# Attention followed by a mixture of experts: the attention's tiles in phases of three pairs, and GpSimd's indirect stores behind spaced operations

## The chip, the core and the metric

The kernel runs on one core of a Trainium2 chip. The core has a matrix engine (TensorE, PE in the views), VectorE (DVE), ScalarE (ACT), GpSimd (POOL), and SyncE (SP), which here issues DMAs. Each engine takes its own instructions in its own order, and the engines wait for each other by semaphores. The metric is device time in microseconds of one execution, as a median of several runs. Times inside an execution come from one profiled run and count from the start of its span.

## What is computed

Two parts follow each other. The first is a gated linear attention over 4 batches, 8 heads, 768 positions and a head size of 48. Each position has a complex gate, and a state of 48 x 48 per head is turned, damped and added to:

```python
mag = np.sqrt(a_re * a_re + a_im * a_im)
scale = np.minimum(mag, 0.999) / (mag + 1e-06)
a_re_n, a_im_n = (a_re * scale, a_im * scale)
for t in range(S):
    new_re = ar * S_re - ai * S_im
    new_im = ar * S_im + ai * S_re
    S_re, S_im = (new_re + kv, new_im)
    y[:, :, t] = np.einsum('bhd,bhde->bhe', q[:, :, t], S_re)
```

Its output, 3072 tokens of 384 numbers, is the input of the second part, a mixture of 8 experts with two layers (384 to 1024 to 384). A noisy gate picks two experts for each token:

```python
noisy_logits = logits + noise_scale * noise
top2 = np.argpartition(-noisy_logits, 2, axis=1)[:, :2]
for e in range(E):
    for k in range(2):
        mask = top2[:, k] == e
        h = np.maximum(x[mask] @ w1[e], 0.0)
        out[mask] += top2_w[mask, k, None] * (h @ w2[e])
```

## The kernel before, in words

The attention works on 24 tiles of 128 positions. Tile n belongs to batch b = n mod 4 and tile group g = n div 4, so a group has one tile of each batch and the state goes from group to group. Tiles 2m and 2m+1 make pair m, 0 to 11. The gate's magnitude and angle are handled in pairs, the rest by tile:

- load_a, load_qk, load_v (L485 to L497): DMAs on SP for a pair's gates (re, im) and a tile's q, k and v.
- p1(m) (L505): ScalarE's Ln and Exp with VectorE's products give the log of the magnitude. p2a(m) (L520) is the Arctan, p2carry(m) (L524) adds on VectorE the angle that the group before left in car, p2t(n) (L530) makes prefix sums of the angles on TensorE (cum), rounds them on ScalarE and VectorE into tf and sends tf's last row by DMA to car (L544). p2s(m) (L546) takes Abs and two Sines: tr.
- p3(n) (L557): prefix sums of the logs on TensorE, two Exps on ScalarE (ee), qk times ee on VectorE. p3q(n, i) (L571): VectorE's products qk times tr, which give qh (i = 0) and kh (i = 1).
- tr_unit(n, i) (L577): eight transposes on TensorE into ptr and ScalarE's copy of ptr to qT or kT. sc_unit (L586): scores psc on TensorE, masked by VectorE into am. st_unit, st_upd, st_scale (L598 to L626): the state, z. y_unit (L628): TensorE's pY from z and am, ScalarE's xT; for b = 0 GpSimd opens xr, a buffer of the group's rows (three of them).
- x_unit(n) (L648): transposes back, ScalarE's copy to xr.
- glog, gturn, gsel, gdis, gscat (L656 to L747) are the gates of a group of tiles: logits, a transpose, the choice of two experts (its Exp and Ln on ScalarE), the slot of each token in its expert's list (counts on TensorE, pos and at last the reduction sl at L707 on VectorE), and gscat, which writes the rows of xr by GpSimd's indirect DMA to the slots in xs, two stores for each tile (L715). gscat3_0_4 stands for group 3, tiles 0 to 4 (exclusive); its eight stores are .0 to .7. The groups 4 and 5 go in two parts, 0_3 and 3_4.

The experts' part then reads xs by expert and runs mm1 (ph, or psc where the attention's banks are used, L966), ScalarE's and VectorE's evictions to h (L968, L971), and mm2 (po, L1002). The first pieces of it are mixed into the attention's last tiles; x_T (L926 to L949) and load_w (w1h, w2h, L870) get its operands ready.

ScalarE holds one table at a time, for Exp and Ln or for Arctan and Sine. phase(i, ...) (L464) puts each activation into a numbered phase, even for Exp and Ln, odd for the other, and loads the table at the phase's first use (L467). All of ScalarE's activations of phase i stand between the loads of i and i+1. phase_of(m) gives the phase of a pair.

The order is written out by hand in three tables. EMIT is the order in which the steps are written, so the order of buffers. ORDER holds for PE, ACT, DVE and SP a list of tokens, which is that engine's own order; a token is a step with its numbers and a count of its runs of instructions on that engine, as p2s10.1. PACE (L249) adds waits: the first instruction of one token waits for the last of another. POOL has no list; its order comes out when the kernel is built, from EMIT and the waits.

Of the kernel before, what the change touches and what calls it, by code (L numbers as in the profile page):

```python
# [37 lines left out]
    load_a2 load_qk0 load_qk1 load_a3 load_qk2 p11 p12 p30 p31 load_v0 consts2 load_qk3 p2a0 p2a1 p2t0 p2a2 p2t1  # L38
    load_a4 p2t2 p2t3 p2s0 load_v1 load_qk4 p2s1 p32 load_v2 p3q0_0 load_qk5 load_qk6 tr_unit0_0 p2carry2 p3q1_1
    load_qk7 p13 load_v3 p3q0_1 p3q1_0 load_qk8 tr_unit0_1 p14 p33 load_a5 st_unit0 p2t4 st_upd0 tr_unit1_0 p2t5  # L40
    tr_unit1_1 p3q2_1 sc_unit0_0 st_unit1 p2a3 sc_unit0_1 y_unit0 p3q2_0 clear_out7 tr_unit2_0 clear_out1 p2a4
    load_qk9 p2carry3 p2t6 p2carry4 p2t7 st_upd1 p2s2 sc_unit1_0 p3q3_1 tr_unit2_1 sc_unit1_1 p3q3_0 st_unit2 load_v4
    p2s3 p34 sc_unit2_0 st_upd2 tr_unit3_0 p35 sc_unit2_1 load_a6 y_unit1 p36 tr_unit3_1 load_v5 p3q4_0 y_unit2 p15
    st_unit3 p3q5_0 p37 st_upd3 tr_unit4_0 p3q4_1 sc_unit3_0 p16 p2t8 p3q5_1 tr_unit4_1 load_v6 p2t9 load_a7 st_unit4
    load_qk10 sc_unit3_1 y_unit3 sc_unit4_0 tr_unit5_0 sc_unit4_1 tr_unit5_1 x_unit0 p2a5 glog0_0_4 clear_out9 p3q6_0
    clear_out4 load_qk11 p2carry5 x_unit1 p2s4 load_v7 p2t10 st_scale0 p2t11 st_scale3 y_unit4 st_scale2 sc_unit5_0
    st_scale1 gturn0_0_4 load_v8 tr_unit6_0 p2s5 p3q6_1 x_unit2 load_qk12 sc_unit5_1 st_upd4 y_unit5 p2a6 st_unit5
    p3q7_0 p38 gsel0_0_4 p3q7_1 tr_unit6_1 st_upd5 p39 load_a8 p2carry6 p310 load_qk13 st_unit6 p17 p3q8_0 sc_unit6_0
    p3q8_1 tr_unit7_0 sc_unit6_1 y_unit6 p18 p311 tr_unit7_1 p2t12 sc_unit7_0 st_upd6 tr_unit8_0 load_v9 p2t13 x_unit3
    load_v10 sc_unit7_1 clear_out8 st_unit7 tr_unit8_1 x_unit4 y_unit7 st_upd7 p3q9_1 sc_unit8_0 load_a9 p2a7  # L50
    sc_unit8_1 p3q9_0 load_v11 x_unit5 tr_unit9_0 p2s6 p2carry7 clear_out0 st_unit8 load_qk14 st_scale4 p2t14
    tr_unit9_1 st_scale7 p2t15 p3q10_0 glog1_0_4 clear_out10 sc_unit9_0 y_unit8 p2a8 p3q11_0 p2s7 p2carry8 gturn1_0_4
    tr_unit10_0 st_upd8 p312 p3q10_1 p2t16 sc_unit9_1 st_unit9 st_scale5 p313 load_a10 p2t17 tr_unit10_1 p314
    clear_out5 clear_out2 y_unit9 load_qk15 st_scale6 sc_unit10_0 p19 p3q11_1 load_qk16 load_qk17 x_unit6 load_v12
    tr_unit11_0 gdis0_0_4 gsel1_0_4 p110 sc_unit10_1 p3q12_0 y_unit10 x_unit7 tr_unit11_1 gscat0_0_4 p315 load_a11
    sc_unit11_0 st_upd9 tr_unit12_0 x_unit8 sc_unit11_1 clear_out6 st_unit10 y_unit11 st_upd10 load_v13 p2a9 p3q12_1
    st_unit11 p3q13_0 tr_unit12_1 st_upd11 glog2_0_4 load_qk18 p2carry9 load_qk19 load_v14 p2s8 sc_unit12_0
    tr_unit13_0 p3q13_1 gturn2_0_4 p2t18 st_scale8 p2t19 p2a10 tr_unit13_1 sc_unit12_1 st_unit12 y_unit12 p3q14_0 p2s9
# [1472 lines left out]
```

## Time and profile before

| what | us |
|---|---|
| median of three runs (683.65 to 687.44) | 686.25 |
| the profiled execution's own time | 686.77 |
| its span in the profile | 685.1 |
| TensorE busy in the span | 650.1 |
| VectorE busy | 435.1 |
| ScalarE busy | 367.9 |
| GpSimd busy | 174.9 |

The span lies within the execution's own time. Busy time leaves out waiting; a busy TensorE need not be at its peak, since matmuls are pipelined. Shares over the whole span are means over an attention part, up to about 268 us, and an experts' part, with other limits in each. The granted clock of TensorE stands in the views as a share of its higher level of 2.4 GHz: 1.00 is that, 0.50 is 1.2 GHz, and numbers between are means over a stretch. "remote" or "another core or an unknown queue" as a releaser means that the profile found no event that ended the wait; "issue" means that the engine waited for nothing that the profile shows.

### The profile page before, as it was taken

How to read it: one execution, taken by the hardware profiler on the slowest of the kernel's cores; microseconds unless marked ns; L12 is line 12 of the kernel's file. 1: busy time of each engine (PE TensorE's matmuls, PEld its weight loads, DVE VectorE, ACT ScalarE, POOL GpSimd, SP SyncE). 2: the span in 40 equal slices, each digit the busy share in tenths (PEclk: the TensorE clock that was granted, in tenths of full speed). 3: DMA queues.
4: the chain of work that ended last, by engine and by line, in shares of the span. 5: the costliest groups of instructions: out<-in, count | busy, mean ns of one | idle time of the engine just before them, and what ended most of it. 6: DMA issues, size and time to landing. Idle time of an engine off the chain costs nothing.

```text
span 685.1 us, 14285 instructions
## 1 busy us (share of the span) xinstructions
PE 650.1 (95%) x5505; PEld 573.5 (84%) x5505; DVE 435.1 (64%) x971; ACT 367.9 (54%) x610; POOL 174.9 (26%) x183
## 2 busy tenths in 40 slices
PE   8999999997989788999999999999999999999995
PEld 3468786876878577989899899899899899899895
DVE  7899999987778547546556526735735736746411
ACT  6999999987646345264423622732632732723300
POOL 3000000135230426002513302152142142163311
PEclk9999999999899889999999999999999999999998
DMA  6937766758386555278654756698598697682201
GB/s 240 295 113 205 212 158 211 199 177 258 118 249 182 184 165 171 87 252 236 173 159 118 264 143 203 198 192 223 189 166 250 193 186 228 194 219 91 83 36 35
DMA packets 120012, 124.24 MB, mean 181 GB/s; under 512 B 73610, under 2 KB 99104, under 8 KB 119936
## 3 DMA queue, kind: packets, MB, share of 16 engines
q1 hardware_dynamic: 110672, 95.76, 48.4%
q0 software_dynamic: 9264, 27.48, 13.3%
q8 instruction: 45, 0.74, 0.4%
q14 instruction: 31, 0.25, 0.1%
HBM read 70.11 MB, written 42.90 MB: 165 GB/s over the span
## 4 chain that ended last, share of the span: by engine, by line
PE 77%; DVE 11%; ACT 4%; another core or an unknown queue 2%; DMA 2%; issue 2%; SPq 1%; POOL 0%; POOLq 0%; ACTq 0%
PE ph L966 29%; PE po L1002 24%; PE po L1027 6%; PE ptr L583 3%; PE psc L593 2%; PE cum L533 2%; PE pY L642 2%; PE pY L644 1%; PE psc L966 1%; DVE qk L565 1%; DVE am L594 1%; DVE qh L573 1%; PE cum L652 1%; DVE im L528 1%
## 5 line engine op out<-in xcount | busy, mean ns | idle before, releaser
L966 PE MATMUL ph<-x,w1h 128*128 128x512 f32 (+4 forms) x720 | 184.7, 345 | 0.0
L1002 PE MATMUL po<-w2h,h 128*128 128x384 f32 x640 | 164.2, 335 | 0.0
L966 PEld LDWEIGHTS ph<-x,w1h 128*128 128x128 f32 x720 | 125.2, 188 | 14.9 <-DVE x L949 0.2
L987 POOL DMA_INDIRECT out_dram<-ao,ox x54 | 58.0, 1073 | 258.4 <-DVE ao L1015 155.4
L966 PE MATMUL ph<-x,w1l 128*128 128x512 f32 (+4 forms) x360 | 123.9, 344 | 0.0
L1002 PEld LDWEIGHTS po<-w2h,h 128*128 128x128 f32 x640 | 115.8, 188 | 0.3
L968 ACT ACTIVATE h<-ph 128x512 fp32r<-128x512 f32 (+4 forms) x120 | 60.7, 511 | 101.0 <-PE ph L966 82.2
L971 DVE SCALAR_TENSOR_TENSOR h<-ph,h 128x512 fp32r<-128x512 f32 (+5 forms) x128 | 69.3, 548 | 60.2 <-ACT h L968 55.3
L1002 PE MATMUL po<-w2l,h 128*128 128x384 f32 x320 | 107.0, 334 | 0.0
L715 POOL DMA_INDIRECT xs<-xr,sl x48 | 54.1, 1127 | 201.7 <-DVE kh L573 127.3
L1015 DVE SCALAR_TENSOR_TENSOR ao<-po,gw,ao 128x384 f32<-128x384 f32 (+1 forms) x42 | 25.7, 612 | 101.5 <-PE po L1002 101.3
L966 PEld LDWEIGHTS ph<-x,w1l 128*128 128x128 f32 x360 | 67.6, 188 | 7.6
L948 ACT CAST x<-xj 128x512 fp32r<-128x512 f32 (+4 forms) x39 | 20.7, 531 | 87.1 <-DVE xj L945 86.2
L978 POOL DMA_INDIRECT ao<-out_dram,ox x47 | 54.5, 1160 | 32.5 <-issue 28.8
L1002 PEld LDWEIGHTS po<-w2l,h 128*128 128x128 f32 x320 | 60.1, 188 | 0.2
L593 PEld LDWEIGHTS psc<-qT,kT 112*64 112x64 f32 x768 | 37.6, 143 | 5.9 <-issue 3.9
L593 PE MATMUL psc<-qT,kT 112*64 112x128 f32 (+1 forms) x768 | 41.1, 257 | 1.1 <-ACT kT L584 0.6
L644 PE MATMUL pY<-am,v 128*48 128x128 f32 x384 | 37.2, 277 | 5.0 <-issue 2.3
L594 DVE TENSOR_TENSOR am<-psc,mask 128x512 f32<-128x512 f32 x48 | 32.3, 680 | 13.6 <-PE psc L593 7.2
L1027 PE MATMUL po<-h,w2h 128*128 128x272 f32 (+2 forms) x192 | 38.7, 294 | 0.0
L949 DVE TENSOR_TENSOR x<-xj,x 128x512 fp32r<-128x512 f32 (+4 forms) x39 | 22.6, 579 | 24.1 <-ACT x L948 24.1
L584 ACT ACTIVATE kT<-ptr 112x1024 f32<-112x1024 f32 x24 | 24.8, 1032 | 22.7 <-remote 14.8
(246 smaller groups left out, 1113.4 us busy)
## 6 DMA issues: line engine op xcount, KB each, us to landing
raw<-in_moe_w_dram SPq DMA_DIRECT2D x24, 512.0 KB
raw<-in_moe_w_dram SPq DMA_DIRECT2D x32, 384.0 KB
qk<-in_qk_dram SPq DMA_DIRECT2D x24, 384.0 KB
v<-in_v_dram SPq DMA_DIRECT2D x24, 288.0 KB
xgb<-xs SPq DMA_DIRECT2D x8, 800.0 KB
xp<-xp SPq DMA_DIRECT2D x7, 768.0 KB
re<-in_a_dram SPq DMA_DIRECT2D x12, 384.0 KB
im<-in_a_dram SPq DMA_DIRECT2D x12, 384.0 KB
```

What stands on the lines that cost most here:

```text
L593: nc.tensor.matmul(p[o:o + 64, j, z:], KT[n][:, h, z:z + 64], QT[n][:, h, z:], start=True, stop=True, skip_group_check=True)
L594: nc.vector.tensor_mul(AM[n][:, 4 * half:4 * half + 4, :].rearrange("p (a r) t -> p a (r t)", r=2), p.rearrange("p (a r) t -> p a (r t)", ...
L644: nc.tensor.matmul(o, V[n][:, H + h // 2 if h % 2 else h, :], AM[n][:, h, :], start=not g, stop=True, skip_group_check=True)
L715: d = nc.gpsimd.indirect_dma_start(out=xs, out_offset=bass.IndirectOffsetOnAxis(ap=sl[:, kk, b:b + 1], axis=0), in_=XR[g][:, lo + b, :], i ...
L966: nc.tensor.matmul(p[:, :n], W1[e, kk][i][:, f * 128:(f + 1) * 128], XW[w, kk][:, j, :], start=(c == 0), stop=(c == len(ms) - 1))
L968: highs.append(nc.scalar.activation(h[:, 0:n], p[:, :n], AF.Relu))
L971: d = nc.vector.scalar_tensor_tensor(h[:, dst:dst + b - a], p[:, a:b], 0.0, h[:, a:b].bitcast(F32), op0=OP.max, op1=OP.subtract)
L978: nc.gpsimd.indirect_dma_start(out=ao[j][0:w, :], out_offset=None, in_=out, in_offset=bass.IndirectOffsetOnAxis(ap=OX[e][0:w, j:j + 1], ax ...
L987: d = nc.gpsimd.indirect_dma_start(out=out, out_offset=bass.IndirectOffsetOnAxis(ap=OX[e][0:n, j:j + 1], axis=0), in_=a, in_offset=None, b ...
L1002: nc.tensor.matmul(p[:, :DM], HT[w, f][i][:, o:o + 128], W2[f // 2][k2][:, f % 2, :], start=(m == 0), stop=(m == len(ms) - 1))
L1015: kept.append(nc.vector.scalar_tensor_tensor(a, p[0:n, :DM], g, a, op0=OP.mult, op1=OP.add))
L1027: nc.tensor.matmul(p[:, :n], W2[f // 2][k2][:, f % 2, kk * 128:(kk + 1) * 128], HT[0, f][i][:, 0:n], start=(m == 0), stop=(m == len(ms) - 1))
```

## The change

Pairs go three to a phase and not two, after a first phase of three in both; the phases of Sines, Exps of ee and gates follow:

```diff
     def load_a(m):
-        RE[m] = pf.tile([128, 2, HD], F32, name="re", bufs=4)
-        IM[m] = pf.tile([128, 2, HD], F32, name="im", bufs=4)
+        RE[m] = pf.tile([128, 2, HD], F32, name="re", bufs=5)
+        IM[m] = pf.tile([128, 2, HD], F32, name="im", bufs=5)
...
     def phase_of(m):
-        return 0 if m < NP0 else 2 * ((m - NP0 + 2) // 2)
+        return 2 * (m // 3)
+
+
+    def turn_phase(m):
+        return 1 if m < 2 else min(2 * ((m + 1) // 3) + 1, 7)
...
-        phase(2 * (2 * m // B) + 1, flat(TR[m][:, 0]), a, AF.Sin, scale=-TWO_PI, bias=b_cos)
-        phase(2 * (2 * m // B) + 1, flat(TR[m][:, 1]), f, AF.Sin, scale=-TWO_PI)
+        phase(turn_phase(m), flat(TR[m][:, 0]), a, AF.Sin, scale=-TWO_PI, bias=b_cos)
+        phase(turn_phase(m), flat(TR[m][:, 1]), f, AF.Sin, scale=-TWO_PI)
...
-        ph = 2 * g + 2 if n > 1 else 0
+        ph = 2 * ((n + 4) // 6) if n > 1 else 0
...
-                   lambda *a: phase(2 * min(g + 3, NG), *a),
+                   lambda *a: phase((4, 6, 6, 8, 8, 8)[g], *a),
```

Phases 0 to 12 become 0 to 8, so 13 table loads become 9. EMIT and ORDER are written anew up to about tile 19, to match; the experts' part keeps its order. In PACE the three waits of TensorE stay, and GpSimd's stores get other ones. Before, the stores of groups 0 to 2 stand in orders of their own (.1, .3, .6, .7 and so on for group 0), and some stores have no such wait; after, they stand as .0, .1, .2, and each later one has its own operation of ScalarE or VectorE. Only the last store of group 5's first part (gscat5_0_3.5) now stands behind those of its second part. The rows for group 3 and the first of group 4:

```diff
 PACE = {
...
-    ("POOL", "gscat2_0_4.3"): ("ACT", "y_unit17.0"), ("POOL", "gscat3_0_4.1"): ("ACT", "tr_unit19_0.0"),
-    ("POOL", "gscat3_0_4.0"): ("ACT", "load_w10.0"), ("POOL", "gscat3_0_4.5"): ("ACT", "glog4_0_3.0"),
-    ("POOL", "gscat3_0_4.3"): ("ACT", "gsel4_0_3.1"), ("POOL", "gscat3_0_4.7"): ("ACT", "x_T0_0_1.0"),
-    ("POOL", "gscat3_0_4.2"): ("ACT", "gsel4_0_3.2"), ("POOL", "gscat3_0_4.6"): ("ACT", "x_unit18.0"),
...
+    ("POOL", "gscat2_0_4.7"): ("DVE", "p3q19_1.0"), ("POOL", "gscat3_0_4.1"): ("ACT", "x_T0_0_1.0"),
+    ("POOL", "gscat3_0_4.2"): ("ACT", "x_T0_0_2.0"), ("POOL", "gscat3_0_4.3"): ("DVE", "gsel4_0_3.14"),
+    ("POOL", "gscat3_0_4.4"): ("ACT", "mm10_0_1.0"), ("POOL", "gscat3_0_4.5"): ("DVE", "st_scale17.0"),
+    ("POOL", "gscat3_0_4.6"): ("ACT", "y_unit20.0"), ("POOL", "gscat3_0_4.7"): ("ACT", "tr_unit22_1.0"),
+    ("POOL", "gscat4_0_3.0"): ("ACT", "y_unit21.0"), ("POOL", "gscat4_0_3.1"): ("DVE", "gsel4_3_4.11"),
```

Line numbers of after are two to five higher than those of before. ScalarE before, the phase of the Arctans of pairs 3 and 4, from its table load to the next. im is the angle, tr<-tf are Sines (tf, small where a bias is given):

```order
L467 ACT_TABLE_LOAD
L468 ACTIVATE im<-im 128x768
L584 ACTIVATE qT<-ptr 112x1024
L645 ACTIVATE xT<-pY 128x512
L468 ACTIVATE tr<-tf 128x768
L468 ACTIVATE im<-im 128x768
L538 ACTIVATE tf<-cum,small 128x384 x2
L468 ACTIVATE tr<-tf,small 128x768
L584 ACTIVATE kT<-ptr 112x1024
L468 ACTIVATE tr<-tf,small 128x768
L468 ACTIVATE tr<-tf 128x768
L467 ACT_TABLE_LOAD
```

ScalarE after, the phase of the Arctans of pairs 3 to 5, its first rows:

```order
L469 ACT_TABLE_LOAD
L470 ACTIVATE tr<-tf,small 128x768
L470 ACTIVATE tr<-tf 128x768
L470 ACTIVATE im<-im 128x768 x2
L650 ACTIVATE xT<-pY 128x512
L589 ACTIVATE qT<-ptr 112x1024
L543 ACTIVATE tf<-cum,small 128x384 x2
L470 ACTIVATE im<-im 128x768
L589 ACTIVATE kT<-ptr 112x1024
L470 ACTIVATE tr<-tf,small 128x768
L543 ACTIVATE tf<-cum,small 128x384 x2
L470 ACTIVATE tr<-tf 128x768
```

And on to the next load:

```order
L555 ACTIVATE tf<-tf 128x768
L650 ACTIVATE xT<-pY 128x512
L589 ACTIVATE qT<-ptr 112x1024
L543 ACTIVATE tf<-cum,small 128x384
L470 ACTIVATE tr<-tf,small 128x768
L470 ACTIVATE tr<-tf 128x768
L543 ACTIVATE tf<-cum,small 128x384
L469 ACT_TABLE_LOAD
```

Between two loads stood 11 operations with two Arctans; now 21 with three stand there, and three pairs of Sines.

GpSimd before, the stores of group 3 (sl_2899) and the first of group 4, with what each waits for by engine or DMA queue:

```order
L715 DMA xs<-xr,sl_2899 24576x400 [waits DVE_49,Activation_49,Pool_49]
L715 DMA xs<-xr,sl_2899 24576x400
L715 DMA xs<-xr,sl_2899 24576x400 [waits Activation_49]
L715 DMA xs<-xr,sl_2899 24576x400 x5
L715 DMA xs<-xr,sl_3339 24576x400 [waits DVE_49,DMASW0_49,Activation_49,Pool_49]
L715 DMA xs<-xr,sl_3339 24576x400 [waits DMASW1_49]
L715 DMA xs<-xr,sl_3339 24576x400 [waits DMASW2_49]
```

GpSimd after, the same stores (sl_2895 is group 3's, sl_3335 that of group 4):

```order
L720 DMA xs<-xr,sl_2895 24576x400 [waits DVE_49,Activation_49,Pool_49]
L720 DMA xs<-xr,sl_2895 24576x400 [waits Activation_49] x2
L720 DMA xs<-xr,sl_2895 24576x400 [waits DVE_49]
L720 DMA xs<-xr,sl_2895 24576x400 [waits Activation_49]
L720 DMA xs<-xr,sl_2895 24576x400 [waits DVE_49]
L720 DMA xs<-xr,sl_2895 24576x400 [waits Activation_49] x2
L720 DMA xs<-xr,sl_3335 24576x400 [waits DVE_49,DMASW0_49,Activation_49,Pool_49]
L720 DMA xs<-xr,sl_3335 24576x400 [waits DMASW1_49,DVE_49]
L720 DMA xs<-xr,sl_3335 24576x400 [waits DMASW2_49,Activation_49]
```

Six of the eight stores of group 3 waited for nothing that the one ahead did not; now seven have each a wait of their own.

VectorE before, around the reduction that gives group 3's slots (sl_2899; qh, kh are products of p3q, h evictions of the experts' first matmuls):

```order
L573 TENSOR_TENSOR kh_124<-qk,tr 128x2x8x48
L313 TENSOR_SCALAR ga3e<-ga3w_3117 128x3
L922 CAST ox<-xga 128x3
L304 MAX_INDEX ga3ix<-ga3mx,ga3c 128x8
L573 TENSOR_TENSOR qh_122<-qk,tr 128x2x8x48
L304 MAX_INDEX ga3ix<-ga3mx,ga3c 128x8
L971 SCALAR_TENSOR_TENSOR h_3252<-psc_140,h_3252 128x256
L314 RECIPROCAL ga3w_3117<-ga3e 128x3
L315 TENSOR_TENSOR ga3w_3117<-ga3w_3117 128x3
L306 TENSOR_TENSOR ga3oh<-iota_85,ga3ix 128x48
L707 TENSOR_REDUCE sl_2899<-ga4oh 128x8
```

VectorE after, where that reduction (sl_2895) now stands:

```order
L875 TENSOR_TENSOR w1l_2849<-raw,w1h_2848 128x1024
L285 SCALAR_TENSOR_TENSOR ga3c<-lz 128x24
L578 TENSOR_TENSOR kh_123<-qk,tr 128x2x8x48
L320 TENSOR_TENSOR xr<-ga4t 128x4x8
L706 TENSOR_TENSOR pos_2891<-cum,base_run 128x32
L708 TENSOR_TENSOR base_run<-base_run,cum 128x8
L709 TENSOR_TENSOR ga4oh<-ga4oh,pos_2891 128x64
L712 TENSOR_REDUCE sl_2895<-ga4oh 128x8
```

The reduction stood behind evictions of the experts' h and gate steps of group 4, in row 414 of VectorE; it now stands in row 376, right behind the kh product and the three steps that lead to it.

## Rows read from the trace of the kernel before

**Rows 1.** The page's chain that ended last, share of the span by engine.

```profile
PE 77%; DVE 11%; ACT 4%; another core or an unknown queue 2%; DMA 2%; issue 2%; SPq 1%; POOL 0%; POOLq 0%; ACTq 0%
```

**Rows 2.** Stretches: us; busy PE, PEld, DVE, ACT, POOL (instructions); clock; DMA share; GB/s.

```profile
80.00:100.00 20.00, 20.00 (x306) 16.58 (x302) 19.84 (x43) 19.55 (x34) 0.00 (x0) 1.00 0.56 144
...
120.00:140.00 20.00, 18.63 (x314) 16.11 (x313) 16.70 (x46) 17.53 (x29) 5.63 (x5) 1.00 0.74 202
...
160.00:180.00 20.00, 16.18 (x234) 13.06 (x234) 13.38 (x31) 12.35 (x18) 7.85 (x9) 0.83 0.60 186
...
220.00:240.00 20.00, 15.05 (x156) 11.55 (x156) 11.64 (x45) 8.49 (x15) 8.44 (x9) 0.86 0.51 177
...
300.00:685.00 385.00, 377.38 (x2190) 355.00 (x2188) 194.69 (x362) 149.83 (x251) 112.50 (x101) 1.00 0.63 173
```

**Rows 3.** The chain in order of time: start, us, what.

```profile
15.97 1.28 ACT L467
...
45.07 1.57 PE cum L533 x4
...
50.56 1.28 ACT L467
...
164.83 4.53 DMA v<-in_v_dram
...
170.37 2.93 PE cum L533 x4
...
179.55 1.02 PE ptr L583 x8
...
227.72 8.76 another core or an unknown queue
...
237.57 1.97 PE ptr L583 x8
...
240.74 5.89 another core or an unknown queue
...
268.34 8.45 PE po L1002 x48
```

**Rows 4.** Timeline of VectorE, 163 to 170: start, us, operation [idle before, releaser].

```profile
163.45 0.95 DVE L573 TENSOR_TENSOR kh<-qk,tr 128x768 f32<-128x768 f32 x1
...
169.03 0.19 DVE L701 TENSOR_TENSOR pos<-cum,base_run 128x32 f32<-128x32 f32 x1 [4.07 <-remote]
```

**Rows 5.** Timeline of TensorE, 227 to 233.

```profile
227.18 1.09 PE L583 MATMUL ptr<-ident,kh 128*112 128x128 f32 x8
...
232.75 0.42 PE L644 MATMUL pY<-am,v 128*48 128x128 f32 x4 [1.23 <-issue]
```

**Rows 6.** Timeline of GpSimd, the first and the last of eight stores.

```profile
224.83 1.16 POOL L715 DMA_INDIRECT xs<-xr,sl  x1 [18.23 <-DVE ohs L688]
...
233.95 0.97 POOL L715 DMA_INDIRECT xs<-xr,sl  x1 [0.30 <-issue]
```

**Rows 7.** Stretches of 4 us, the columns as in rows 2.

```profile
164.00:168.00 4.00, 2.85 (x57) 2.53 (x53) 0.96 (x3) 2.55 (x3) 3.22 (x4) 1.00 1.12 335
...
228.00:232.00 4.00, 2.38 (x23) 1.19 (x21) 0.80 (x2) 0.00 (x0) 3.09 (x4) 1.00 0.44 172
232.00:236.00 4.00, 1.55 (x8) 0.66 (x8) 3.65 (x15) 0.00 (x0) 2.31 (x3) 0.78 0.74 235
...
272.00:276.00 4.00, 4.00 (x25) 4.00 (x24) 3.97 (x10) 0.88 (x2) 3.22 (x4) 1.00 0.82 300
```

**Rows 8.** Table loads by line (ns, min/median/max), and timeline rows of ScalarE.

```profile
L467 ACT ACT_TABLE_LOAD  x13: 1283/1283/1283, 0.8 to 183.0; - x13
...
17.26 2.31 ACT L468 ACTIVATE im<-im 128x768 f32<-128x768 f32 x3
...
214.45 0.43 ACT L948 CAST x<-ptr 128x320 fp32r<-128x320 f32 x1 [0.90 <-PE ptr L939]
...
236.50 1.02 ACT L584 ACTIVATE kT<-ptr 112x1024 f32<-112x1024 f32 x1 [8.78 <-remote]
```

More of the change, by code (lines that the diff above doesn't have):

```diff
@@ L42 @@
[L42 to L46, printed above, removed]
@@ new lines @@
+    st_upd15 st_scale12 tr_unit17_1 gturn3_0_4 y_unit16 st_scale13 gsel3_0_4 st_unit16 p3q18_0 load_v17 p321 p322
+    load_qk23 p323 sc_unit17_0 p3q18_1 sc_unit17_1 p3q19_0 x_unit12 st_scale14 tr_unit18_0 st_upd16 close_f
+    clear_out11 tr_unit18_1 st_unit17 y_unit17 load_v18 picked load_w10 st_scale15 sc_unit18_0 x_unit13 p3q19_1
+    gdis3_0_4 tr_unit19_0 st_upd17 sc_unit18_1 x_unit14 load_v19 tr_unit19_1 st_unit18 load_x0_0 y_unit18 p3q20_1
+    p3q21_0 load_v20 sc_unit19_0 p3q20_0 load_v21 sc_unit19_1 load_v22 tr_unit20_0 x_unit15 gscat3_0_4 glog4_0_3
@@ new lines @@
+    tr_unit20_1 gturn4_0_3 y_unit19 gsel4_0_3 p3q22_0 x_unit16 st_upd18 x_T0_0_0 sc_unit20_0 p3q22_1 x_T0_0_1
+    glog4_3_4 sc_unit20_1 st_unit19 st_upd19 x_T0_0_2 gturn4_3_4 x_unit17 st_upd23 x_unit18 gsel4_3_4 mm10_0_1
+    st_scale16 y_unit20 tr_unit21_0 p3q21_1 mm10_0_2 tr_unit21_1 gdis4_0_3 gscat4_0_3 x_G0_0 p3q23_0 tr_unit22_0
+    p3q23_1 sc_unit21_0 st_scale17 x_unit19 tr_unit22_1 sc_unit21_1 y_unit21 tr_unit23_0 gdis4_3_4 sc_unit22_0
+    st_scale18 sc_unit22_1 tr_unit23_1 st_scale19 y_unit22 sc_unit23_0 load_v23 sc_unit23_1 gscat4_3_4 glog5_0_3
@@ L120 @@
+        mm11_0_6.0 x_T0_1_0.0 x_T0_1_1.0 mm11_0_7.0 x_T0_1_2.0 mm10_1_0.0 mm10_1_1.0 mm10_1_2.0 mm10_1_3.0 mm10_1_4.0
+        mm10_1_5.0 mm10_1_6.0 mm10_1_7.0 mm20_1_3.0 mm20_1_4.0 mm20_1_5.0 mm20_1_6.0 mm11_1_0.0 mm11_1_1.0 mm11_1_2.0
+        mm11_1_3.0 mm11_1_4.0 mm11_1_5.0 mm21_0_0.0 mm21_0_1.0 mm11_1_6.0 mm21_0_2.0 mm11_1_7.0 mm21_1_3.0 mm21_1_4.0
+        mm21_1_5.0 mm21_1_6.0
     """,
     "ACT": """
[L122 removed]
@@ new lines @@
+        mm10_0_6.0 gsel5_0_3.2 x_unit20.0 y_unit23.0 mm10_0_0.0 mm10_0_3.0 x_unit21.0 glog5_3_4.0 mm10_0_4.0
+        gsel5_3_4.0 gsel5_3_4.1 x_unit22.0 load_w11.0 gsel5_3_4.2 mm10_0_7.0 x_unit23.0 load_w11.2 load_w11.1
+        x_T1_0_2.0 x_T1_0_0.0 x_T1_0_1.0 mm11_0_1.0 mm11_0_2.0 mm11_0_3.0 mm11_0_0.0 mm11_0_4.0 mm11_0_5.0 mm11_0_6.0
+        x_T0_1_0.0 x_T0_1_1.0 x_T0_1_2.0 mm20_0_2.0 mm11_0_7.0 mm10_1_0.0 mm10_1_1.0 mm10_1_2.0 x_P1_1.0 x_P1_1.3
+        x_P1_1.2 x_P1_1.1 mm10_1_5.0 x_P2_0.1 mm10_1_3.0 mm10_1_4.0 x_P2_0.0 load_w12.0 load_w12.1 mm10_1_6.0
@@ new lines @@
+        p2t13.0 p2t12.0 p313.0 p3q10_1.0 gsel0_0_4.14 gsel0_0_4.18 st_upd8.0 p3q11_0.0 gsel0_0_4.13 p2t14.0
+        st_scale7.0 gsel0_0_4.19 p2t15.0 st_upd11.0 p2carry8.0 p3q10_0.0 gsel0_0_4.11 gsel0_0_4.12 sc_unit9_0.0
+        st_scale5.0 gsel0_0_4.15 p3q11_1.0 p2t16.0 p3q12_0.0 gturn1_0_4.0 sc_unit9_1.0 gsel0_0_4.20 gsel1_0_4.0
+        gsel1_0_4.1 gsel1_0_4.2 st_upd9.0 p2t17.0 gsel1_0_4.3 gsel0_0_4.21 gsel1_0_4.4 gsel0_0_4.22 p3q12_1.0
+        gsel1_0_4.5 sc_unit10_0.0 gsel1_0_4.6 gdis0_0_4.0 gsel1_0_4.7 gsel1_0_4.10 p19.0 p19.1 sc_unit10_1.0
@@ new lines @@
+        load_w10.1 load_w10.2 p323.2 load_v21.0 load_x0_0.0 load_x0_0.1 p322.2 p321.2 load_v22.0 p322.1
+        load_w20_0_1_2.0 load_w20_0_1_2.1 load_w20_0_1_2.2 gscat3_0_4.0 load_v23.0 gscat4_0_3.0 load_x1_0.0
+        load_x1_0.1 load_w20_3.0 load_w11.0 load_w11.1 load_w11.2 x_S1.0 x_S1.1 x_S1.2 x_S1.3 x_S1.4 x_S1.5
+        gscat4_3_4.0 gscat5_3_4.0 gscat5_0_3.0 load_x0_1.0 ranked.0 ranked.1 ranked.2 ranked.3 ranked.4 ranked.5
+        ranked.6 ranked.7 ranked.8 ranked.9 ranked.10 ranked.11 load_x1_1.0 load_w12.0 load_w12.1 load_w12.2
@@ L247 @@
+        load_x2_0.0 x_P1_1.0 clear_out3.0 load_x2_0.1 x_L1_1.0 x_L1_1.1 x_L1_1.2 x_L1_1.3 x_L1_1.4 x_L1_1.5
+        load_x2_1.0 load_w21.0 load_w21.1 load_w21.2 x_P2_0.0 load_w21.3 x_L2_0.0 x_L2_0.1 x_L2_0.2 x_L2_0.3 x_L2_0.4
+        x_L2_0.5 x_P2_1.0 x_L2_1.0 x_L2_1.1 x_L2_1.2 x_L2_1.3 x_L2_1.4 x_L2_1.5
     """,
```

342 lines of the change are left out of this document (158 added, 184 removed), and 32 rows, old and new, of the table PACE.

## Prediction

> **What bounds the kernel now.** I read the chain of work that ended last first: TensorE has 77% of it, VectorE 11%, ScalarE 4%, and a releaser that the profile can't name 2% [rows 1]. So there are stages with other limits than TensorE. The table of stretches shows three kinds [rows 2]. From 80 to 100 TensorE, VectorE and ScalarE are all over 97% busy: there nothing is gained without taking work away. From 160, and again from 220, all three have idle time together, and the granted clock falls to 0.83 and 0.86. From 300 to the end TensorE is busy for 377.4 of 385 us at the full clock. The chain has its first long piece of pure matmuls at 268.34 [rows 3]. So the change, which leaves the experts' part as it is, can earn only by letting that part begin earlier. A microsecond saved on the path ahead of it is a microsecond of the total.
>
> Second, I looked for what the idle stretches have in common. The chain has three long pieces that are no work: 4.53 us from 164.83, 8.76 us from 227.72 and 5.89 us from 240.74 [rows 3]. The first is put down to the load of v, but the row that waited is VectorE's pos, idle for 4.07 us and released by something unnamed [rows 4], and pos needs only TensorE's counts of the gates (gdis2). The other two are ScalarE waiting for the transposes that fill kT. TensorE had sent out the eight transposes of the first by 228.3, and after them it crawls: it stands idle 1.23 us ahead of four matmuls that take 0.42 us, for nothing but issue [rows 5]. In all three places GpSimd is sending stores of xs: from 224.83 to 233.95 eight of them, one each 1.3 us [rows 6]. In the fine stretches TensorE is busy for 2.85 of 4 us at 164, 2.38 at 228 and 1.55 at 232 while 3 or 4 stores run [rows 7]. The clock was still 1.00 in the first two, so the clock doesn't start it; it falls afterwards. Against this reading stands the stretch at 272: four stores, and TensorE busy for all of 4.00 us, on long matmuls of the experts [rows 7]. So what goes together is many small matmuls and a run of stores, and that the one causes the other is not shown.
>
> **The change part by part.** *Spacing of the stores.* Before, a store waits for its data and in part for an operation that is long over, and a run leaves at GpSimd's own pace. After, each later store waits for an operation of its own. The seven that group 3's stores now wait for ended between 214.9 and 237.5 in before [rows 8], so they stand (237.5 - 214.9) / 6 = 3.8 us apart on the mean, an estimate, as the last gap holds the long wait itself. The group can also begin some 12 us earlier, since the reduction that gives its slots goes up VectorE's order to right behind a kh product. The cost that can go is the three waits: 4.07 + 8.76 + 5.89 = 18.72 us [rows 3, 4]. The bounds are 0 (TensorE loses the same to each store wherever it stands) and 18.72 (it loses nothing to one that stands alone). No row of before has spaced stores beside small matmuls, so I take the middle: **-9.4 us**. Behind a waiting store GpSimd's queue holds the later stores and the memset and copy that open the next xr. The last stores, of group 5, end about where they did, and the matmuls from 268.34 on, 8.45 us of them in one piece, cover what reads them next.
>
> *The clock.* Behind these waits some matmuls run at half the clock: four of the prefix take 2.93 us where a full-clock row of the same four takes 1.57, and eight transposes 1.97 where others take 1.02 [rows 3]. That is 1.36 and 0.95 us at two of the places; for three I estimate 3 x 1.155 = 3.46 us. It goes with the idle time ahead of it, so the bounds are 0 and 3.46, and I take the same half: **-1.7 us**.
>
> *Table loads.* Pairs go three to a phase, so 13 loads of ScalarE's tables become 9. One is 1.283 us [rows 8], four are 5.13 us of ScalarE. Only three of them are on the chain, the first at 15.97 and the last at 50.56 [rows 3]; the first two lead to the first Arctans and out of the first Sines, and these stay. So one lies on the path and can go: **-1.3 us**, bounds 0 and -5.13. The others are hidden behind VectorE, which is as busy as ScalarE from 80 to 100 [rows 2]; if its work ran out there, the bound of 5.13 would hold.
>
> The Trainium skill, page "ScalarE: Activation LUTs", section "What ACT_TABLE_LOAD costs", gives a load 1283 ns and about 1380 ns of drain besides. The load's length agrees; the trace shows no drain behind it, since the activation after the load of 15.97 starts at 17.26 [rows 3, 8]. By the page the one load on the chain would be an estimated 2.66 us, and the sum 1.4 us lower.
>
> *The longer phases.* ScalarE's trig group of pairs 3 to 5 has three Arctans and three pairs of Sines, 21 operations between its two loads, where the group of pairs 3 and 4 had 11 (both stand in the section on the change). Within it a carry goes from tile to tile: the last row of tf goes by a DMA on SP to car, VectorE adds it to the next pair's angles, and TensorE's prefix matmuls wait for that. If it shows, one such joint costs a DMA's landing; the nearest row, of a loaded moment, has 4.53 us [rows 3], and the three full groups would have 13.6. What covers it: the transposed copies (1.02 us each [rows 8]) that stand in the group, and VectorE's products of 0.95 us [rows 4] for other tiles; five of them cover one joint, and about that many stand there. The opposite bound is a gain: the re-made order could fill idle time of VectorE, 3.3 of 20 us from 120 to 140 [rows 2]. I take a loss of a third of one joint, nearer to covered than to shown, since VectorE has other work all through: **+1.5 us**, bounds -3.3 and +13.6.
>
> *No cost.* VectorE has the same instructions in another order. The fifth buffer of re and im lets loads start earlier, and SP's DMAs carry the same bytes; what hides them is the 160 us of attention ahead. Without that cover a load would be at most the 4.53 us above.
>
> Sum against the profiled execution: 686.77 - 9.4 - 1.7 - 1.3 + 1.5 = 675.9 us. The median of the runs shown, 686.25, is 0.5 below the profiled one, so as a median **675.4 us**.
>
> **The rivals.** *A, stores cost the same everywhere, or aren't the cause.* TensorE's gaps stay and only one load goes: 686.25 - 1.3 + 1.5 = 686.5 us. For it: the stretch at 272, where stores and a full TensorE go together [rows 7]; and from 120 to 140 five stores ran with TensorE at 18.63 of 20 us [rows 2]. Against it: TensorE is idle for (4 - 2.38) + (4 - 1.55) = 4.07 of 8 us from 228, a stretch that begins at the full clock [rows 7].
>
> The Trainium skill, page "SBUF — State Buffer", under "SBUF: two separate sides", says that a DMA never contends with a compute engine, and that TensorE and ScalarE never wait on anyone. By that rule spaced stores would bring nothing and A would hold. The trace's gaps of TensorE at a full clock beside a run of stores [rows 5, 7] speak against its holding here, but don't refute it, since what holds TensorE there has no name.
>
> *B, slower.* While a trig group runs no Exp can run, and VectorE's qk, qh and kh products need Exp's results. A group of 21 operations in the place of 11 is 10 longer; at 0.9 us each (0.77 for an Arctan, 1.02 for a transposed copy [rows 8]) that is 9.0 us. With no stock of products at all VectorE would starve that long in each of three full groups. B decides from (9.4 + 1.7 + 1.3) / 3 = 4.1 us of starving a group on; midway from there to 9.0, at 6.5 us, it gives 686.25 - 9.4 - 1.7 - 1.3 + 3 x 6.5 = 693.4 us. For it: from 80 to 100 VectorE is 99% busy, so each starved microsecond counts [rows 2]. Against it: the Exps of three pairs now stand ahead in one phase, which makes the stock larger too.
>
> *C, the spacing doesn't take.* The operations waited for may be over when a store's own data comes, and the stores of group 3 then leave in a run as before. The wait of 8.76 us stays with its clock loss of 0.95, and half of the rest goes: 686.25 - (18.72 - 8.76)/2 - (3.46 - 0.95)/2 - 1.3 + 1.5 = 680.2 us.
>
> **How the numbers follow.** Forecast 0.48, C 0.15, A 0.20, B 0.17. A measurement of this kernel can tell about 0.5%, 3.4 us, from no change. The forecast and C lie on the faster side (0.63), A within (0.20), B on the slower (0.17). The forecast's own range is 663 to 680. Its lower end has all of the waits and the clock's excess gone, and one load: 686.25 - 18.72 - 3.46 - 1.28 = 662.8. The wide range must take in C, A and the near part of B, so it goes up to A with one joint of the carry shown: 686.25 - 1.28 + 4.53 = 689.5. That leaves out some 0.11 of B above, and 0.06 below for a case in which all four loads and VectorE's idle time count too.
>
> **What would show it.** Right: 9 table loads; stores of xs 2 us and more apart from 130 to 275; no unnamed wait of over 2 us ahead of kT; a granted clock of about 1.00 from 160 to 260; the piece of 48 matmuls of po, now at 268.34, some 11 us earlier, and the part behind it as long as before. A shows as spaced stores with TensorE's gaps still there. B shows as VectorE idle ahead of qk, waiting for ScalarE's ee, between 45 and 190, with the part behind unchanged. C shows as stores 1.3 us apart around 215 to 235. The prediction is wrong in its core if TensorE's gaps go but the experts' part starts no earlier: then loads of weights or the gates' own chain had been next to late.

## The result and the profile after

The changed kernel took 675.19 us (median of six runs, 673.04 to 680.33), against 685.99 us for the kernel before on the same chip (683.65 to 688.15). The ratio is 0.9836, with a 95% interval of 0.9804 to 0.9868. The forecast was 675.4 us. The total came out as forecast, but its terms didn't, as the experiments below show.

The page's chain that ended last, share of the span by engine, of the changed kernel:

```profile
PE 84%; DMA 4%; DVE 4%; SPq 3%; ACT 2%; issue 1%; POOL 0%; POOLq 0%; DVEq 0%; ACTq 0%
```

The unnamed releaser, 2% in [rows 1], is gone; DMAs and SP's issues have come in. Stretches of the changed kernel, with the columns of [rows 2]:

```profile
60.00:80.00 20.00, 16.68 (x197) 12.02 (x198) 18.32 (x30) 17.30 (x27) 0.00 (x0) 1.00 0.49 128
...
180.00:200.00 20.00, 17.93 (x239) 14.36 (x239) 15.22 (x49) 10.75 (x21) 11.02 (x11) 0.94 0.57 188
220.00:240.00 20.00, 20.00 (x295) 18.08 (x294) 17.10 (x62) 12.92 (x21) 9.93 (x9) 1.00 0.75 256
240.00:260.00 20.00, 19.02 (x154) 17.64 (x153) 14.65 (x76) 11.85 (x28) 10.83 (x11) 1.00 0.78 210
...
300.00:671.00 371.00, 363.74 (x2122) 342.77 (x2121) 187.47 (x347) 141.29 (x239) 110.06 (x98) 1.00 0.62 172
```

From 220 to 240 TensorE is now busy all the time at the full clock, where [rows 2] had 15.05 of 20 us at 0.86. From 60 to 80 it is busy for only 16.68. GpSimd's timeline of the changed kernel, stores of group 3, and the table loads by line:

```profile
215.09 0.99 POOL L720 DMA_INDIRECT xs<-xr,sl  x1 [11.76 <-DVE ga3c L290]
216.56 1.21 POOL L720 DMA_INDIRECT xs<-xr,sl  x1 [0.48 <-issue]
219.51 0.98 POOL L720 DMA_INDIRECT xs<-xr,sl  x1 [1.74 <-ACT x L953]
222.04 1.44 POOL L720 DMA_INDIRECT xs<-xr,sl  x1 [1.55 <-DVE ga3e L313]
```

```profile
L469 ACT ACT_TABLE_LOAD  x9: 1283/1283/1283, 0.8 to 181.9; - x9
```

The group begins at 215.09 where [rows 6] had 224.83, its stores stand 1.5 to 3 us apart, and nine loads are left. Three pieces of the changed kernel's chain:

```profile
66.75 3.33 DMA car<-tf
...
158.97 3.75 DMA car<-tf
...
254.76 8.43 PE po L1007 x48
```

The 48 matmuls of po start 13.58 us earlier than in [rows 3], 254.76 against 268.34. The experts' part behind them is as long as before, so the whole gain was made ahead of it. Laid side by side by ScalarE's evictions of y, the two profiled runs were even for long: tile 20's ended at 227.0 before and 228.7 after, 1.7 us later, tile 21's at 238.7 and 232.5, and tile 23's at 259.3 and 247.0. On balance all of the gain of this pair of runs came behind 227 us. The two car pieces are new on the chain: they are the joint of the longer phases. Of the signs set ahead, two fell short: many stores stand less than 2 us apart, those of group 2 1.3 to 2.0, and from 180 to 200 the clock is 0.94.

### The profile page after: what moved, and what is told of

It reads as the page before. It is cut to its first block, busy times and chain, and to the rows that moved or that the text cites. A ratio compares the mean times of both kernels' runs of the same rounds, so it can differ in the third digit from the quotient of the medians.

```text
span 671.3 us, 14276 instructions
## 1 busy us (share of the span) xinstructions
PE 644.7 (96%) x5502; PEld 569.8 (85%) x5505; DVE 435.9 (65%) x971; ACT 363.1 (54%) x606; POOL 179.2 (27%) x183
## 3 DMA queue, kind: packets, MB, share of 16 engines
q0 software_dynamic: 9264, 27.48, 13.5%
## 4 chain that ended last, share of the span: by engine, by line
PE 84%; DMA 4%; DVE 4%; SPq 3%; ACT 2%; issue 1%; POOL 0%; POOLq 0%; DVEq 0%; ACTq 0%
PE ph L971 29%; PE po L1007 25%; PE po L1032 6%; PE ptr L588 5%; PE psc L598 4%; PE pY L647 3%; PE pY L649 2%; PE cum L565 2%; PE cum L657 2%; PE psc L971 2%; PE pG L610 1%; DMA out_dram<-none 1%; DMA im<-in_a_dram 1%; DMA car<-tf 1%; PE cum L538 1%
## 5 line engine op out<-in xcount | busy, mean ns | idle before, releaser
L971 PEld LDWEIGHTS ph<-x,w1h 128*128 128x128 f32 x720 | 125.2, 188 | 14.8 <-DVE x L954 0.2
L720 POOL DMA_INDIRECT xs<-xr,sl x48 | 58.7, 1223 | 185.4 <-DMA v<-in_v_dram 132.3
L983 POOL DMA_INDIRECT ao<-out_dram,ox x47 | 56.0, 1191 | 32.3 <-issue 28.9
L598 PEld LDWEIGHTS psc<-qT,kT 112*64 112x64 f32 x768 | 36.0, 137 | 7.8 <-issue 7.0
L954 DVE TENSOR_TENSOR x<-xj,x 128x512 fp32r<-128x512 f32 (+4 forms) x39 | 22.6, 579 | 22.2 <-ACT x L953 21.5
L647 PE MATMUL pY<-qT,z 112*48 112x128 f32 x320 | 32.1, 278 | 1.0 <-issue 0.7
```

Of the source, the lines that this page charges most:

```text
L598: nc.tensor.matmul(p[o:o + 64, j, z:], KT[n][:, h, z:z + 64], QT[n][:, h, z:], start=True, stop=True, skip_group_check=True)
L647: nc.tensor.matmul(o, Z[b][:, h, :], QT[n][:, h, :], start=True, stop=False, skip_group_check=True)
L720: d = nc.gpsimd.indirect_dma_start(out=xs, out_offset=bass.IndirectOffsetOnAxis(ap=sl[:, kk, b:b + 1], axis=0), in_=XR[g][:, lo + b, :], i ...
L971: nc.tensor.matmul(p[:, :n], W1[e, kk][i][:, f * 128:(f + 1) * 128], XW[w, kk][:, j, :], start=(c == 0), stop=(c == len(ms) - 1))
L983: nc.gpsimd.indirect_dma_start(out=ao[j][0:w, :], out_offset=None, in_=out, in_offset=bass.IndirectOffsetOnAxis(ap=OX[e][0:w, j:j + 1], ax ...
```

## Experiments

They ran on several chips, and this has to be told first: the kernel before took 685.99 us on the chip of the record, 687.68 and 688.10 us on chip 14, but 660.36 us on chip 9 and 660.34 us on chip 2. The two figures of chip 14 belong to two series of runs, so differences across them can be off by their 0.4 us. Each kernel is therefore compared with a before on its own chip, and differences are taken within one chip; two chips stand side by side only where the text says so.

### Chip 9: stores in runs, and a control

The changed kernel without the new waits, for the groups 3 to 5 alone and then for all:

```diff
-    ("POOL", "gscat3_0_4.1"): ("ACT", "x_T0_0_1.0"),
-    ("POOL", "gscat3_0_4.2"): ("ACT", "x_T0_0_2.0"),
...
-    ("POOL", "gscat5_0_3.5"): ("ACT", "x_T1_0_0.0"),
```

> The changed kernel without the new waits of GpSimd's stores of the groups 3, 4 and 5; phases, orders and the earlier slots of group 3 stay. Spacing theory: stores of group 3 leave 1.3 us apart again, TensorE stands beside them and the time goes back by the 12 to 15 us gained behind 227 us: 685 to 690 us. Rival, phases and orders earned it: 675 us as the changed kernel. Rival, the earlier slots earned it: 675 us.

> The changed kernel with none of the waits of GpSimd's stores. Spacing theory: as with the groups 3 to 5 unspaced, and some 0 to 7 us more for the stores of the groups 0 to 2, which then leave in three runs beside small matmuls between 138 and 200 us: 685 to 697 us. Rival, phases and orders: 675 us.

They took 668.93 and 668.52 us, 1.0138 of before (1.0102 to 1.0174, and 1.008 to 1.0195). And the kernel before with parts of the change; first slots early and stores spaced, then slots early alone:

```diff
     "DVE":
-        ... p3q22_1.0 gdis3_0_4.0 ... gdis3_0_4.1 ... gdis3_0_4.2 ... gdis3_0_4.3 ...
+        ... p3q22_1.0 gdis3_0_4.0 ... gdis3_0_4.1 gdis3_0_4.2 gdis3_0_4.3 ...
 PACE = {
+    ("POOL", "gscat3_0_4.1"): ("ACT", "x_T0_0_1.0"),
...
+    ("POOL", "gscat5_0_3.5"): ("ACT", "x_T1_0_0.0"),
```

> The kernel before with two edits alone: group 3's slot reduction and the step ahead of it right behind the first steps of that count in VectorE's order, and the changed kernel's waits for the stores of the groups 3 to 5. Spacing theory: all of the gain, since up to 227 us the two kernels stand within 2 us: 671 to 676 us. Rival, phases and orders: 684 to 687 us.

> The kernel before with group 3's slot reduction early in VectorE's order alone, stores unspaced. Spacing theory: the run of eight stores leaves at about 212 us, 1.3 us apart, and TensorE's gaps move with it; the second run from 239 stays: 680 to 688 us. Rival, the earlier slots earned it: 672 to 677 us.

They took 659.93 us (0.9998 of before, 0.9988 to 1.0007) and 660.38 us (1.0, 0.9991 to 1.001). None of the numbers expected fits as written, since all were set from a before of 686 us. On this chip there is nothing for spacing to gain. The stretches of the kernel before with slots early, on chip 9, show why; its eight stores of group 3 leave from 201.52 to 212.68, 1.3 to 2.0 us apart, and the four from 205.24 to 209.08 1.28 us apart:

```profile
204.00:208.00 4.00, 4.00 (x42) 3.85 (x42) 3.25 (x14) 1.75 (x5) 3.09 (x4) 1.00 0.82 257
208.00:212.00 4.00, 4.00 (x45) 3.73 (x45) 3.38 (x15) 3.02 (x7) 3.39 (x3) 1.00 1.06 400
```

Four and three stores in 4 us, and TensorE busy for all of it, where [rows 7] had 2.38 and 1.55. So on this chip a run of stores doesn't stop TensorE. What is left here is the rest of the change: with phases and orders, and without any waits of the stores, the kernel is 8.2 us slower than before (668.52 - 660.36), although four loads are gone.

### Chip 14: the changed kernel again, and spacing alone

> The changed kernel as it is, once more, on a chip where the kernel before is measured beside it. If the time of before depends on the chip (686 us where it was recorded, 660 us where the first experiments ran), then: on a chip with before near 660 us, the phases and orders show alone and the changed kernel has 667 to 670 us, slower than before; on a chip with before near 686 us, 675 us again. Rival, the chips differ by a common factor: 0.984 of before on each.

The changed kernel took 676.94 us (673.82 to 678.28) against 688.10, a ratio of 0.9831 (0.9773 to 0.9889): chip 14 behaves as the chip of the record. In the next kernel the one before got the early slots and all of the new waits, with none of the phases and orders.

```diff
 PACE = {
-    ("POOL", "gscat0_0_4.7"): ("ACT", "p315.1"), ("POOL", "gscat0_0_4.1"): ("ACT", "p110.2"),
...
+    ("POOL", "gscat0_0_4.1"): ("DVE", "sc_unit11_1.0"), ("POOL", "gscat0_0_4.2"): ("ACT", "p316.1"),
...
```

> The kernel before, with group 3's slot reduction early and the changed kernel's waits for all stores, groups 0 to 5. Theory, stores in runs cost TensorE time on some chips only: on a chip with before near 686 us 662 to 676 us, on one with before near 660 us 659 to 664 us. Rival, spaced stores cost something themselves: over 664 us on the latter.

It took 664.76 us (664.33 to 665.53), 0.965 of before (0.9594 to 0.9706). Spaced stores with early slots are worth 23.3 us there, more than the whole change, and this kernel beats both: it is 12.2 us faster than the changed one beside it. Its chain has the experts' po at 246.50, and one unnamed piece left:

```profile
186.19 2.29 another core or an unknown queue
...
246.50 8.43 PE po L1030 x48
```

The other way round, the changed kernel without its waits for stores, the same kernel as on chip 9:

> The changed kernel with none of the waits of GpSimd's stores, as in the first experiments, now beside a chip's before. Theory: on a chip with before near 688 us TensorE's gaps come back and the kernel has 690 to 702 us, the cost of the phases and orders on top of before; on one with before near 660 us, 668.5 us again.

It took 698.93 us (692.09 to 700.36), 1.0134 of before (1.006 to 1.0207). So spacing gives 698.93 - 676.94 = 22.0 us within the changed kernel too, and without it the kernel is 11.3 us slower than the 687.68 of before. The two gains have different starting points: the 22.0 us are against no waits at all, the 23.3 against the waits and the late slots of before. One kernel on two chips is the clearest view. Its chain on chip 14, and 4 us of the run of group 3's stores there, 232.34 to 237.43 one each 1.27 us:

```profile
230.65 2.58 another core or an unknown queue
234.56 5.26 another core or an unknown queue
```

```profile
232.00:236.00 4.00, 3.12 (x19) 2.44 (x20) 3.01 (x12) 1.01 (x3) 2.94 (x4) 1.00 1.02 366
236.00:240.00 4.00, 1.79 (x14) 1.53 (x12) 1.27 (x6) 0.15 (x1) 1.94 (x2) 1.00 0.94 353
```

And on chip 9, where the run stood at 214.56 to 221.65:

```profile
216.00:220.00 4.00, 4.00 (x36) 3.75 (x37) 3.06 (x16) 2.09 (x6) 3.08 (x4) 1.00 1.06 395
220.00:224.00 4.00, 4.00 (x67) 3.63 (x64) 3.97 (x17) 2.44 (x4) 2.31 (x2) 1.00 0.82 301
```

The DMA engines move as much on the chip where TensorE isn't held (395 GB/s) as where it is (366), so the bytes moved alone don't decide. What does differ between the chips, no run here shows.

### Chip 14: late slots

The kernel with spacing, but with the slot reduction of group 3 where it was.

> The kernel before with the changed kernel's waits for all stores, and group 3's slots where they were in VectorE's order. If the earlier slots matter since the stores of group 3 otherwise leave in a run when their waits are over: 670 to 678 us on a chip with before near 688. If the waits alone do it: 663 to 667 us as with the earlier slots.

It took 672.49 us (672.34 to 673.57), 7.7 us more than with the early slots, as the first theory says. GpSimd's timeline, the chain, and two stretches:

```profile
221.54 0.97 POOL L737 DMA_INDIRECT xs<-xr,sl  x1 [0.30 <-issue]
222.82 0.97 POOL L737 DMA_INDIRECT xs<-xr,sl  x1 [0.31 <-issue]
```

```profile
220.47 7.27 another core or an unknown queue
```

```profile
220.00:224.00 4.00, 2.58 (x25) 1.65 (x24) 0.81 (x2) 0.47 (x1) 2.93 (x3) 1.00 0.40 154
224.00:228.00 4.00, 1.71 (x13) 1.35 (x15) 1.78 (x6) 0.24 (x1) 1.95 (x2) 0.52 0.40 154
```

When the slots came, the operations that the stores wait for were over; seven stores left in a run and one wait of 7.27 us stands in the chain. This is rival C's mechanism: waits space nothing if the stores' data comes after them.

### Chip 14: the price of a table load

```diff
             phases[i] = [nc.scalar.preload_act_table_set(("natural_log_exp_and_others", "trig_and_small")[i % 2])]
+            if i in (4, 8):
+                phases[i].append(nc.scalar.preload_act_table_set("trig_and_small"))
+                phases[i].append(nc.scalar.preload_act_table_set("natural_log_exp_and_others"))
```

> The kernel before with group 3's slots early and all stores spaced (664.8 us where before is near 688), and four table loads more on ScalarE, two at the third load of Exp's table and two at the fifth, each 1.283 us. This prices what the change takes away. Loads on the path: 5.1 us slower than the same kernel without them. Loads hidden behind VectorE, as the prediction has it: 0 to 2 us slower.

It took 670.10 us (669.50 to 670.52), 5.3 us more than the 664.76 without the loads. The loads by line:

```profile
L505 ACT ACT_TABLE_LOAD  x13: 1283/1283/1283, 0.8 to 181.7; - x13
L507 ACT ACT_TABLE_LOAD  x2: 1283/1283/1283, 51.7 to 116.5; - x2
L508 ACT ACT_TABLE_LOAD  x2: 1283/1283/1283, 53.0 to 117.8; - x2
```

Four loads of 1.283 are 5.13 us, so each shows at its whole length. By ScalarE's evictions of y the kernel is 2.3 us late from tile 1 on and 4.9 us from tile 8 on, and that stays to the end. The first two stand behind a load that was on the chain already ([rows 3] has it at 50.56). The other two tell more. In the kernel without them the chain has no piece of ScalarE from 105 to 134; here is one piece of it at that place, with the stretch around it, in which three engines are full:

```profile
116.81 0.94 PE ptr L611 x8
```

```profile
114.00:120.00 6.00, 6.00 (x67) 4.71 (x64) 6.00 (x13) 5.90 (x13) 0.00 (x0) 1.00 0.44 151
```

With them the chain goes through three loads:

```profile
115.23 1.28 ACT L505
116.52 1.28 ACT L507
117.80 1.28 ACT L508
```

So these two, at a place off the chain, still cost 2.5 us of their 2.57, and weren't hidden behind VectorE. The four loads that the change takes away stand at other places; that each of them was worth as much isn't shown.

### Chip 14: two tries at the longer phases

First the clears of the output, eleven writes of 384 KB that SP issues early in the changed kernel:

```diff
     "SP":
-        ... load_a3.0 clear_out4.0 load_qk0.0 clear_out9.0 load_a2.1 load_qk1.0 ...
+        ... load_a3.0 load_qk0.0 load_a2.1 load_qk1.0 ... load_qk11.0 ...
```

> The changed kernel with the eleven early clears of the output (384 KB each, written from zeros) moved back in SP's order, each behind the same load of q and k as in before. In the changed kernel three pieces of the chain up to 62 us are DMAs, two of them such clears. Theory, the clears ahead of the loads of gates delay the first tiles: 3 to 8 us faster than the changed kernel on the same chip. Rival, the longer phases themselves cost the time: within 1.5 us of it.

It took 674.41 us (673.50 to 676.81) beside the changed kernel's 676.94 (673.82 to 678.28). The runs overlap, and the profiled spans are 672.4 and 672.1 us: no clear difference, and at best a small part. The clears stand on the chain in the profile of the result, but not in that of the changed kernel on chip 14. Then the carry, as VectorE waited for it:

```diff
     "DVE":
-        ... st_upd3.0 p2carry5.0 p36.0 p3q6_0.0 sc_unit4_0.0 ...
+        ... st_upd3.0 p36.0 p3q6_0.0 sc_unit4_0.0 p2carry5.0 ...
```

> The changed kernel with VectorE's carry of pair 5 (p2carry5) moved behind the three operations that follow it there, a product qk, a product qh and a mask of scores. In the changed kernel VectorE idles 3.3 us ahead of that carry for the DMA to car. Theory, the joint of the longer phase costs what VectorE waits: 2 to 3.3 us faster than the changed kernel on the same chip type (677 us where before is near 688). Rival, ScalarE's and TensorE's rows of the group are late by the joint anyway: within 1 us of it.

It took 676.19 us (673.56 to 679.01), 0.75 us less than the changed kernel, within the spread. VectorE's and ScalarE's timelines of the changed kernel on chip 14, with the waits of the joint:

```profile
71.05 0.95 DVE L533 SCALAR_TENSOR_TENSOR im<-car,im 1x768 f32<-1x768 f32 x1 [3.31 <-DMA car<-tf]
```

```profile
73.69 0.58 ACT L543 ACTIVATE tf<-cum,small 128x384 f32<-128x384 f32 x1 [3.75 <-PE cum L538]
```

and with the carry moved:

```profile
71.49 0.95 DVE L539 SCALAR_TENSOR_TENSOR im<-car,im 1x768 f32<-1x768 f32 x1 [0.83 <-DMA car<-tf]
```

```profile
73.49 0.58 ACT L549 ACTIVATE tf<-cum,small 128x384 f32<-128x384 f32 x1 [3.19 <-PE cum L544]
```

VectorE's wait shrank from 3.31 to 0.83 us, ScalarE's only from 3.75 to 3.19, and the time stayed. So what VectorE waits at this joint isn't its price. That the price comes through ScalarE's group, which can't end before the third pair's Sines, fits these waits and isn't shown by a run of its own; in the profile of the result the same two waits are 1.51 and 1.31 us. The joints of the other two groups weren't changed. The chain of that kernel names the DMA, 1.5 KB that took 5 us to land:

```profile
66.44 5.02 DMA car<-tf
```

### Chip 2: wider spacing

In the kernel with spacing alone, VectorE waited 2.32 us ahead of a mask of TensorE's scores near 186 us, released by something unnamed, while stores stood 1.3 to 2 us apart. The stores of the groups 1 and 2 got later operations to wait for:

```diff
+    ("POOL", "gscat2_0_4.2"): ("ACT", "tr_unit18_1.0"), ("POOL", "gscat2_0_4.3"): ("DVE", "sc_unit17_1.0"),
+    ("POOL", "gscat2_0_4.4"): ("ACT", "x_unit13.0"), ("POOL", "gscat2_0_4.5"): ("DVE", "sc_unit18_1.0"),
```

> The kernel before with group 3's slots early and all stores spaced, now with the stores of the groups 1 and 2 about 3 us apart (each behind a later operation than in the changed kernel, in the order .0 to .7), where they were 1.3 to 2 us apart between 180 and 188 us and VectorE waited 2.3 us for TensorE. If the distance of the stores sets what TensorE loses: 660 to 663 us on a chip with before near 688 us, against 664.8 us. Rival, what is left there isn't the stores': 664 to 666 us. On a chip with before near 660 us: 659 to 661 us.

It took 663.97 us against 660.34, a ratio of 1.0053 (1.0039 to 1.0067), above what was expected of such a chip. The chip can't tell what the distance gains if runs of stores cost nothing on it, which its time of before suggests and no run on it shows. It does tell that this kernel, all its waits together, is 3.6 us slower than before there. How much of that the narrower spacing would cost there isn't known: on chip 9 it ran for the groups 3 to 5 alone. Whether the wider one would gain on chip 14 stays open.

## Why the prediction came out, point by point

The total was right, and of its four terms the spacing, the loads and the longer phases were not; the clock was measured only together with the spacing. On chip 14:

| term | predicted | measured | how |
|---|---|---|---|
| stores' waits, early slots and the clock behind them | -11.1 | -23.3 | 664.76 - 688.10; -22.0 for the waits within the changed kernel |
| four table loads | -1.3 | -5.3 | four loads more, at other places |
| longer phases and orders | +1.5 | +17.5 | the rest: 676.94 - 664.76 + 5.3 |
| sum | -10.9 | -11.2 | 676.94 - 688.10 |

The sum holds by construction, since the third row is what is left. That row is also the least sure: by the fastest runs it is 673.82 - 664.33 + 5.3 = 14.8, and by chip 9 an estimated 8.2 + 5.3 = 13.5.

**What bounds the kernel.** Right. The experts' part kept its length, and the change paid only by letting it begin earlier.

**Spacing.** The mechanism was right for the chip of the record and chip 14, and the failed step is "so I take the middle". The upper end of the bounds, 18.72 + 3.46 = 22.2 us, is about what it gave. The stalls weren't spread over the stores; they went where the stores stood 1.5 to 3 us apart, and with them the halved clock: 1.00 from 220 to 260. From 180 to 200, with stores 1.3 to 2 us apart, TensorE is still idle for 2.07 of 20 us at 0.94. The step from slots early was right too and is needed, worth 7.7 us. That a run of stores holds TensorE isn't a property of the kernel alone, though: the prediction didn't consider that it may do so on some chips only.

**Table loads.** The failed step is "The others are hidden behind VectorE". The chain names one releaser at each step, and where three engines are all over 95% busy, as from 114 to 120, two loads that weren't on the chain delayed the kernel by 2.5 us. If the loads that the change removes stood as these did, the bound of 5.13 was the answer. On the skill's account of a load (the Trainium skill, "ScalarE: Activation LUTs", "What ACT_TABLE_LOAD costs"): by its 2.66 us, a load and a drain, four would have been an estimated 10.6 us. Measured was 5.3, the loads alone; the added ones stand right behind another load, with no activation between.

**Longer phases.** The failed step is "nearer to covered than to shown, since VectorE has other work all through". The joint was named rightly, and its size was near: car's landing has 3.33 and 3.75 us on the chain of the changed kernel and 5.02 in an experiment, against 4.53 taken. But ScalarE waits at the joint too, 3.75 us, and what VectorE does meanwhile doesn't shorten that. What was measured, 13.5 to 17.5 us, lies at the bound of 13.6, three joints, or above it, and not near 1.5. How it falls on joints and new orders isn't settled; moving the clears changed nothing clear. The evictions of y on chip 14 show where it stands: against the kernel with spacing alone the changed kernel is 2.0 us ahead at tile 2 and 1.1 ahead at tile 14, 6.6 us late at tile 15, in the last of the three long groups, and 9.0 at tile 23. On chip 9, with no new waits in either, it is also 9.0 late at tile 23. So the start is no loss, and by these rows the time isn't lost in three equal steps. On chip 14 the kernel with spacing alone has tile 20's at 220.4, and before has it at 227.0 on the chip of the record: spacing gained ahead of 227 us too, and the longer phases took it back there.

**Rivals.** A, that stores cost nothing, is false on chip 14 and, by its gaps and its gain, on the chip of the record, and true on chip 9. The rule behind it (the Trainium skill, "SBUF — State Buffer", "SBUF: two separate sides") fits chip 9; on chip 14 the same kernel has 1.79 of 4 us of TensorE beside such a run, which speaks against it there and doesn't say what holds TensorE. B, a starved group, was to decide from 4.1 us a group on. Its size came: over three groups that is 12.4 us, and the longer phases and orders cost more, so with the gains as forecast the kernel would have been no faster. Its sign did not: in the changed kernel's profiles VectorE has no wait ahead of qk between 45 and 190, and its longest there is for the DMA to car. C held for the kernel with late slots alone.

So a forecast that missed by 0.2 us held two errors of about the same size: 12.2 us and 4.0 us of gain left out, and some 16 us of cost. That they cancelled was luck.

## What to carry to other kernels

Undo each part of a change on the chip even where the total came out as forecast; here one half of it, without the other, is 12 us faster than both. Where several engines are all but full, don't price a removed instruction at nothing because it isn't on the chain: here two such loads cost nearly their whole length. Ask of a longer serial group which engine has to wait inside it, not whether some engine has other work. Compare kernels beside their own before on the same chip: the same wait can be there on one chip and not on another.

## What the runs showed that was not expected

The same kernel takes 660.4 us on two chips and 686 to 688 on two others. The difference stands in the attention part: on chip 9 the po piece of the kernel before with early slots stands at 241.70, against 268.34 in [rows 3], and the part behind it is as long. It begins with the stores: tile 11's y is evicted at 133.9 and 134.5, even, the first store leaves at 132.62 and 133.15, and at tile 23 the two stand at 234.0 and 259.3. On chip 14 and the chip of the record TensorE starts only 8 to 25 matmuls in 4 us, at a granted clock of 1.00 at first, while GpSimd sends group 3's stores 1.3 us apart; on chip 9 it does not slow under the same stores. Spacing those of the groups 3 to 5 costs nothing on chip 9 (0.9998 of before); spacing all of them, with the early slots, gains 3.5% on chip 14. It doesn't close the whole gap: tile 23's y stands at 238.7 there, 4.7 us behind the 234.0 of chip 9.
